# Where Silu's activation table is loaded in a fused HGRN2 attention and SwiGLU kernel

## The chip, the core and the metric

The kernel runs on one core of a Trainium2 chip. The metric is the device time of one execution in microseconds, smaller being better, given as the median over runs. Names of engines: PE is the matmul engine (TensorE), PEld its weight load, DVE the vector engine, ACT the scalar engine with its activation tables, POOL the GpSimd engine and SP the engine whose queue issues most transfers.

## The reference

Inputs are q, k, v and f_logit of shape (4, 8, 768, 48), that is batch, heads, time and head dimension, and three weight matrices of a gated feed-forward layer. The attention is a linear recurrence with a gate per channel; its output, with heads side by side, goes through the feed-forward layer.

```python
f = 1.0 / (1.0 + np.exp(-f_logit))
for t in range(S):
    state = f[:, :, t, :, None] * state + np.einsum('bhd,bhe->bhde', k[:, :, t], v[:, :, t])
    y[:, :, t] = np.einsum('bhd,bhde->bhe', q[:, :, t], state)
x = y.transpose(0, 2, 1, 3).reshape(B * S, H * D)          # (3072, 384)
g = x @ w_gate                                             # (384, 1536)
out = (g * (1.0 / (1.0 + np.exp(-g))) * (x @ w_val)) @ w_out   # (1536, 384)
```

So a sigmoid is needed for the gate f, and a Silu for the feed-forward layer. On ACT these two functions use different tables.

## The kernel before

Time is cut into six chunks of 128 steps; chunk c of batch b is a unit. The four units of a chunk make the 512 tokens of one feed-forward block, so there are six blocks, 0 to 5. While PE multiplies for block c, the attention of chunk c + 1 (and the beginning of chunk c + 2) is worked in between.

Block 0 uses plain products (lines 746 to 770). The blocks 1 to 5 (`mlp_fifteen`, lines 908 to 1028) compute gate and value with 15 products per group of columns where the plain way has 18, at the price of sums before and after. There are four such groups, called triples; each runs its products 0 to 14 in the order of the list PRODUCTS (lines 897 to 901). A product accumulates into a bank named A, B, o or c, with gate and value side by side, 512 columns. Because product 3, 6, 9, 12 and 14 all add to the same bank A, ACT first has to copy the running sum out ("aside" or "c11", "c12" and so on, line 959); DVE adds or subtracts the copies (lines 855 and 858). When one of six results is complete, `finish` (line 965) puts it on a list; later products take it off, apply Silu to the gate half on ACT (line 970) and let DVE multiply by the value half (line 906). The first two results, c12 and c22, get their Silu right after the matmuls of products 9 and 10, ahead of the copies of these products.

Then the block goes its way down (`down_seven`, lines 1030 to 1122): 14 half steps of matmuls with w_out, in which ACT only copies two results (lines 1072 and 1079) and issues two output transfers (line 1062). At its end `token_sums` (line 916) prepares on DVE the sums of tokens that the next block's products take.

The attention of a unit (`attention`, lines 528 to 704) is a generator, and each `yield` ends a step. Its first step is the sigmoid of its f logits, for chunks from 2 on in place in a room called fsquares (line 555). The next steps are transposes on DVE (561, 568, 599), scans of the gates (572, 596), the scores on PE (615), their mask on DVE (628), y on PE (649 and 653, or 674), the copy of y towards xT (657 and transfers 664, or 689), and the update of the state. There is one room each for f, k and q: the next unit's transfers are issued by `load_after` once the q transpose of the unit before is written down (line 600).

The order is written out by hand. A clock called now advances by 0.86 for each product and by 1.95 for each half step of the way down, which makes 78.9 for a block ("whole"). `times(c)` (line 835) gives for each unit of chunk c at what value of this clock each step is due, counted from the start of block c - 1, and the main loop (lines 1271 to 1280) lets the steps that are due come in ahead of the next product or half step. From a mark on (line 1248), each engine executes its instructions in that written order. What was written before the mark, the end of block 0 included, is placed by the framework's scheduler.

The first entry of each unit's due times is its sigmoid: for chunk 2 at 0, and then at the due times of the scores of the unit before; for chunk 3 at -14 for b = 0 (that is 64.9 in the block before) and 0.80 for b = 1; for the chunks 4 and 5 at -21.51 for b = 0 and -7.86 for b = 1. An activation whose function is not in the table at hand gets a table load put ahead of it, which shows in the profile as ACT_TABLE_LOAD under the line of that activation.

Of the kernel before, what the change touches and what calls it, by code (L numbers as in the profile page):

```python
# [9 lines left out]
FP32 = mybir.dt.float32  # L10
I32 = mybir.dt.int32
U32 = mybir.dt.uint32
AF = mybir.ActivationFunctionType
# [276 lines left out]
def short_path(ctx, tc, ident, least, judge, q, k, v, f_logit, moe_w_gate, moe_w_val, moe_w_out, out):  # L290
# [9 lines left out]
    nc = tc.nc  # L300
# [14 lines left out]
    SQUARES = 2  # L315
    assert TB <= 512 and DM % 128 == 0 and D <= W

    const = ctx.enter_context(tc.tile_pool(name="const", bufs=1))
# [44 lines left out]
    def pairs(t, off=0):  # L363
        return t[:, off:off + HP * N1].rearrange("p (a t) -> p a t", t=N1)
# [4 lines left out]
        nc.vector.memset(t, 1.0)  # L369
    nc.vector.memset(least, 1.0)  # L370

    states = [const.tile([128, HP, D], FP32, tag=f"state{b}", name=f"state{b}") for b in range(B)]


# [32 lines left out]
    def squares(nm):  # L407
        return rooms[nm][:, Q:Q + HP * RUN].rearrange("t (a i e) -> t a i e", a=HP, i=NI)[:, :, :, 0:Q]
# [119 lines left out]
    def attention(u):  # L528
        b, c = units[u]
# [17 lines left out]
        def transposed(name, src):  # L547
            p = bank(name)
            for a in range(HP):
                nc.tensor.transpose(p[:, a * C:(a + 1) * C],  # L550
                                    src[:, 2 * a:2 * a + 2, :].rearrange("t r d -> t (r d)"), ident)
            return p.rearrange("p (a t) -> p a t", t=C)

        if c >= SQUARES:
            nc.scalar.activation(squares("f"), squares("f"), AF.Sigmoid)
        else:
            p = transposed("fTp", fr)
            nc.scalar.activation(pairs(gate)[:, :, 1:N1], p, AF.Copy if u in ahead else AF.Sigmoid)
# [15 lines left out]
        whole = pairs(tail)[:, :, 1:2]  # L574
# [92 lines left out]
        else:  # L667
# [15 lines left out]
            for par in range(2):  # L683
                for n in range(DM // Q):
                    h = n // per * 2 + par
                    at = n * Q - h * D
# [25 lines left out]
    def attention_steps(c):  # L712

        runs = [attention(c * B + b) for b in range(B)]
        parts = [3, 6, 3, 3]
        order = sorted((2 * b + s, b, n) for b in range(B) for s, n in enumerate(parts))
        return [lambda b=b, n=n: [next(runs[b]) for _ in range(n)] for _, b, n in order]
# [101 lines left out]
    def chain(k, q, qmul, turn=None, head=None):  # L819
        return (*[k + t for t in STEPS], turn or k + 3.5, head or k + 3.5, q, qmul)  # L820

    whole = NJ * TRIPLE + 7 * DOWN
    between = [n * TRIPLE - 0.05 for n in range(NJ)]
    down = [NJ * TRIPLE + n * DOWN / 2 - 0.05 for n in range(14)]
    SCORES = {c: scores for c, scores in zip(range(2, NCH), (
        ((12, "b"), (between[2], "o"), (down[2], "A"), (down[6], "A")),
        ((PRODUCT - 0.05, "b"), (between[1], "o"), (between[3], "o"), (down[3], "A")),
        *[((down[10] - whole, "A"), (between[1], "o"), (between[3], "o"), (down[3], "A"))] * (NCH - 4)))}
# [6 lines left out]
    def times(c):  # L835
        at = [t for t, _ in SCORES[c]]
        outputs = [*at[1:], down[10] if c + 1 in SCORES and SCORES[c + 1][0][0] < -1 else LAST]
        sigmoid = [-14 if c == 3 else SCORES[c - 1][-1][0] - whole - 0.01 if c > 3 else 0, *[t - 0.01 for t in at]]
        masks = {"b": 2, "o": 0.9, "A": 1.5}
        return [[f, *steps, s + 0.02, s + masks[kind], s + 2.2, o, o + 0.01, o + 2.1]  # L840
                for f, steps, (s, kind), o in zip(sigmoid, CHAINS[c], SCORES[c], outputs)]
# [321 lines left out]
    mark = traced[-1]  # L1163
    keep_warm(5)
    first = [attention(b) for b in range(B)]
    done = [0] * B

# [82 lines left out]
    for c in range(2, NCH):  # L1250
        for b in range(B):
            run = attention(c * B + b)
            waiting += [((c - 2) * whole + t, lambda run=run: next(run)) for t in times(c)[b]]
# [33 lines left out]
def kernel(  # L1287
# [22 lines left out]
    def judge(bank):  # L1310
# [12 lines left out]
        yield  # L1323

    short_path(tc, ident, least, judge, *args)
    with tc.If(redo[0] > 0):
        general_path(tc, *args)
# [32 lines left out]
```

## Time and profile before

| | |
|---|---|
| time, median of 8 runs | 615.09 us (614.3 to 615.52) |
| the profiled execution | 615.41 us, span 613.6 us |
| PE busy | 597.0 us (97%) |
| DVE busy | 499.1 us (81%) |
| ACT busy | 285.4 us (47%), 526 instructions |
| table loads on ACT | 30, each 1283 ns: line 970 12, line 555 11, line 558 4, line 762 3 |
| starts of the blocks 1 to 4 (first product) | 147.99, 247.25, 343.26, 437.12 us |

Times within the profile are microseconds from the start of the span. A row of the timeline has the start, the duration, the engine, the line, the operation with its output and inputs, and how often it ran; in brackets stands how long the engine was idle before it and what ended this ("<-issue" where nothing in the profile did). A row of the waits names who waited for whom, the sum in us, how many times, and the longest. A row of the groups has, after the bar, busy time and the mean of one in ns, then idle time before them. The chain of waits is followed back from the last instruction to what released each one. ACTq, SPq and POOLq are the queues of those engines.

### The profile page before, as it was taken

How to read it: one execution, taken by the hardware profiler on the slowest of the kernel's cores; microseconds unless marked ns; L12 is line 12 of the kernel's file. 1: busy time of each engine (PE TensorE's matmuls, PEld its weight loads, DVE VectorE, ACT ScalarE, POOL GpSimd, SP SyncE). 2: the span in 40 equal slices, each digit the busy share in tenths (PEclk: the TensorE clock that was granted, in tenths of full speed). 3: DMA queues.
4: the chain of work that ended last, by engine and by line, in shares of the span. 5: the costliest groups of instructions: out<-in, count | busy, mean ns of one | idle time of the engine just before them, and what ended most of it. 6: DMA issues, size and time to landing. Idle time of an engine off the chain costs nothing.

```text
span 613.6 us, 10812 instructions
## 1 busy us (share of the span) xinstructions
PE 597.0 (97%) x4036; PEld 489.1 (80%) x4036; DVE 499.1 (81%) x882; ACT 285.4 (47%) x526; POOL 7.6 (1%) x51
## 2 busy tenths in 40 slices
PE   7799999999999999999999999999999999999996
PEld 5644545666888799888899988899988899988895
DVE  7799989878999996989996889996879991566731
ACT  2375646312776520576731376641276730366600
POOL 1000000000000000000000000000000000000000
PEclk9899999999999999999999999999999999999999
DMA  9999582005322144424235344145313100100001
GB/s 150 248 209 284 174 249 79 1 14 154 88 52 68 27 98 109 119 53 96 52 94 125 100 112 110 32 113 117 109 44 91 27 5 10 52 2 2 1 0 58
DMA packets 109142, 54.10 MB, mean 88 GB/s; under 512 B 68760, under 2 KB 102168, under 8 KB 109080
## 3 DMA queue, kind: packets, MB, share of 16 engines
q1 hardware_dynamic: 107064, 50.56, 34.7%
q10 hardware_dynamic: 2016, 2.75, 1.2%
q8 instruction: 34, 0.56, 0.4%
q14 instruction: 28, 0.23, 0.1%
HBM read 44.04 MB, written 6.29 MB: 82 GB/s over the span
## 4 chain that ended last, share of the span: by engine, by line
PE 83%; DVE 7%; DMA 3%; ACT 2%; SPq 2%; issue 2%; POOL 0%; DVEq 0%; ACTq 0%; POOLq 0%
PE o L1053 17%; PE A L954 14%; PE B L954 11%; PE gate L752 5%; PE o L775 5%; PE val L752 5%; PE o L954 5%; PE c L954 4%; PE sc L615 4%; PE o L1116 3%; PE y L653 2%; PE y L674 2%; PE dS L694 1%; SPq L664 1%; PE y L649 1%
## 5 line engine op out<-in xcount | busy, mean ns | idle before, releaser
L954 PE MATMUL A<-xs,w_both 128*128 128x256 f32 x240 | 62.5, 383 | 1.2 <-ACT aside L959 1.2
L1053 PE MATMUL o<-w_out,h 128*128 128x192 f32 x360 | 62.0, 327 | 0.5 <-DVE h L906 0.5
L1053 PEld LDWEIGHTS o<-w_out,h 128*128 128x128 f32 x360 | 58.7, 190 | 1.7 <-DVE h L906 0.8
L959 ACT COPY c<-A 128x512 f32<-128x512 f32 x40 | 23.4, 584 | 66.2 <-PE A L954 59.2
L954 PEld LDWEIGHTS A<-xs,w_both 128*128 128x128 f32 x240 | 44.5, 190 | 9.1 <-ACT aside L959 2.8
L855 DVE TENSOR_TENSOR c<-c,aside 128x512 f32<-128x512 f32 x60 | 41.3, 688 | 9.9 <-ACT aside L959 8.5
L959 ACT COPY aside<-A 128x512 f32<-128x512 f32 x60 | 35.0, 584 | 28.9 <-PE A L954 28.9
L906 DVE TENSOR_TENSOR h<-h,c 128x256 f32<-128x256 f32 x100 | 40.8, 417 | 7.9 <-ACT h L970 7.7
L970 ACT ACTIVATE h<-c 128x256 f32<-128x256 f32 x100 | 39.2, 416 | 9.0 <-DVE c L855 5.8
L858 DVE TENSOR_TENSOR c<-c,aside 128x512 f32<-128x512 f32 x60 | 41.1, 685 | 2.0 <-ACT aside L959 1.8
L954 PE MATMUL B<-xs,w_both 128*128 128x256 f32 x160 | 41.2, 380 | 0.7 <-ACT aside L959 0.7
L1053 PE MATMUL o<-ws,h 128*128 128x192 f32 x240 | 41.5, 328 | 0.2 <-DVE A L628 0.2
L954 PE MATMUL c<-xT,w_both 128*128 128x256 f32 x160 | 41.2, 380 | 0.5 <-DVE c L858 0.5
L954 PE MATMUL A<-xs,extra 128*128 128x256 f32 x160 | 41.2, 380 | 0.0
L954 PE MATMUL B<-xT,extra 128*128 128x256 f32 x160 | 41.1, 379 | 0.0
L959 ACT COPY aside<-B 128x512 f32<-128x512 f32 x60 | 35.1, 585 | 10.5 <-PE B L954 7.0
L628 DVE TENSOR_TENSOR A<-sc,causal 128x512 f32<-128x512 f32 x48 | 30.7, 680 | 11.1 <-PE sc L615 11.1
L1053 PEld LDWEIGHTS o<-ws,h 128*128 128x128 f32 x240 | 39.1, 190 | 0.8 <-DVE A L628 0.4
L858 DVE TENSOR_TENSOR c<-o,c 128x512 f32<-128x512 f32 x40 | 27.6, 691 | 10.2 <-ACT h L970 5.8
L954 PEld LDWEIGHTS B<-xs,w_both 128*128 128x128 f32 x160 | 30.2, 190 | 5.2 <-ACT aside L959 1.1
L954 PEld LDWEIGHTS c<-xT,w_both 128*128 128x128 f32 x160 | 30.2, 190 | 5.1 <-DVE c L858 0.9
L954 PEld LDWEIGHTS A<-xs,extra 128*128 128x128 f32 x160 | 30.3, 190 | 4.4 <-ACT c L959 0.3
(137 smaller groups left out, 1139.6 us busy)
## 6 DMA issues: line engine op xcount, KB each, us to landing
fsquares<-in_f_logit_dram SPq DMA_DIRECT2D x64, 96.0 KB, 2.7
ksquares<-in_k_dram SPq DMA_DIRECT2D x64, 96.0 KB, 2.4
qsquares<-in_q_dram SPq DMA_DIRECT2D x64, 96.0 KB, 2.4
v<-in_v_dram SPq DMA_DIRECT2D x24, 192.0 KB, 3.3
w<-in_moe_w_gate_dram SPq DMA_DIRECT2D x6, 768.0 KB, 6.1
w<-in_moe_w_val_dram SPq DMA_DIRECT2D x6, 768.0 KB, 5.7
w<-in_moe_w_out_dram SPq DMA_DIRECT2D x6, 768.0 KB, 5.7
out_dram<-ob ACTq DMA_DIRECT2D x14, 192.0 KB, 2.5
```

What stands on the lines that cost most here:

```text
L615: nc.tensor.matmul(sc[par][:, a * C:(a + 1) * C], lhsT=kT[r, a, :], rhs=qT[r, a, :], start=True, stop=True)
L628: nc.vector.tensor_tensor(A[:, par], sc[par].rearrange("p (a t) -> p a t", t=C), causal.unsqueeze(1).broadcast_to((128, HP, C)), ALU.mult)
L752: nc.tensor.matmul(p, lhsT=w[:, j, i, :], rhs=xT[c][:, i, :], start=(i == 0), stop=(i == KT - 1))
L775: nc.tensor.matmul(p, lhsT=hidden_tile(h, n // 2)[:, n % 2 * 2 + b // 2, b % 2 * C:(b % 2 + 1) * C], rhs=w_out[:, j, :], start=(n == 0), s ...
L855: nc.vector.tensor_tensor(dst, a, b, ALU.add)
L858: nc.vector.tensor_tensor(dst, a, b, ALU.subtract)
L906: lagging.append(lambda: f(*args))
L954: nc.tensor.matmul(p[name][:, n, :], lhsT=weights_of[a][:, n, j, :], rhs=tokens[b], start=fresh and n == 0, stop=True, skip_group_check=True)
L959: nc.scalar.copy(t, p[name])
L970: nc.scalar.activation(dst, src[:, 0, :], AF.Silu)
L1053: nc.tensor.matmul(p[:, n, :], lhsT=lhsTs[j][:, n * C:(n + 1) * C], rhs=rhs[:, j, :], start=first and j == order[0] and n == 0, stop=j == ...
L1116: nc.tensor.matmul(p, lhsT=hidden_tile(h, j)[:, 2, n * C:(n + 1) * C], rhs=b22[:, j, :], start=j == order[0], stop=j == order[-1])
```

## The change

A tile of one column, "spare", is allocated and zeroed on POOL. After the sigmoid of unit b = 0 of chunk 2, and of unit b = 1 of the chunks 3, 4 and 5, ACT applies Silu to this column in place; nothing reads it. The sigmoid of unit b = 1 of chunk 3 becomes due at -4 where it was due at 0.80: in the way down of block 1, no more in the first triple of block 2. For the chunks 4 and 5 the due times stay.

```diff
@@ short_path
     nc.vector.memset(least, 1.0)

+    spare = const.tile([128, 1], FP32, tag="spare", name="spare")
+    nc.gpsimd.memset(spare, 0.0)
     states = [const.tile([128, HP, D], FP32, tag=f"state{b}", name=f"state{b}") for b in range(B)]
@@ attention
         if c >= SQUARES:
             nc.scalar.activation(squares("f"), squares("f"), AF.Sigmoid)
+            if b == (c > SQUARES):
+
+                nc.scalar.activation(spare, spare, AF.Silu)
         else:
@@ times
-        sigmoid = [-14 if c == 3 else SCORES[c - 1][-1][0] - whole - 0.01 if c > 3 else 0, *[t - 0.01 for t in at]]
+        sigmoid = [-14 if c == 3 else SCORES[c - 1][-1][0] - whole - 0.01 if c > 3 else 0, -4 if c == 3 else at[0] - 0.01, *[t - 0.01 for t in at[1:]]]
```

## The prediction

> **What bounds the kernel now.** I began with the page. The profiled execution took 615.41 us; its span is 613.6, so 1.81 lie around it, and it stands 0.32 above the median of 615.09.
>
> ```profile
> ## 1 busy us (share of the span) xinstructions
> PE 597.0 (97%) x4036; PEld 489.1 (80%) x4036; DVE 499.1 (81%) x882; ACT 285.4 (47%) x526; POOL 7.6 (1%) x51
> ```
>
> TensorE is busy for 97%, ACT for less than half. A change on ACT pays only where TensorE stands still for ACT. So next the waits of TensorE, and the groups of ACT:
>
> ```profile
> PE A L954 <- ACT aside L959: 1.2, 4, 0.3
> L970 ACT ACT_TABLE_LOAD x12 | 15.4, 1283 | 0.2
> L555 ACT ACT_TABLE_LOAD x11 | 14.1, 1283 | 0.2
> ```
>
> Four times a matmul into bank A waits for the copy "aside" on ACT, for 0.3 us each time. Tables are swapped 12 times ahead of a Silu of line 970 and 11 times ahead of a sigmoid of line 555, at 1.283 us. The chain of waits, from 260 us on, is TensorE nearly throughout; it leaves it like this, and again at 445.69:
>
> ```profile
> 350.33 0.88 PE c L954 x4
> 351.84 1.14 ACT L970
> 354.07 1.13 PE A L954 x4
> ```
>
> The piece in the middle is a table load. The timeline shows how it comes between two matmuls:
>
> ```profile
> 351.23 0.59 ACT L959 COPY c<-c 128x512 f32<-128x512 f32 x1 [0.28 <-PE c L954]
> 351.55 0.67 DVE L858 TENSOR_TENSOR c<-c,aside 128x512 f32<-128x512 f32 x1
> 351.84 1.28 ACT L970 ACT_TABLE_LOAD   x1
> 352.76 1.03 PE L954 MATMUL c<-xT,w_both 128*128 128x256 f32 x4
> 353.13 0.42 ACT L970 ACTIVATE h<-c 128x256 f32<-128x256 f32 x1
> 353.46 0.57 ACT L959 COPY aside<-A 128x512 f32<-128x512 f32 x1
> 354.07 1.13 PE L954 MATMUL A<-xs,w_both 128*128 128x256 f32 x4 [0.29 <-ACT aside L959]
> 355.04 1.03 PE L954 MATMUL B<-xT,extra 128*128 128x256 f32 x4
> ```
>
> Copy of c31, load, first Silu, copy of A, all in ACT's order; product 12 adds to bank A and must let that copy read first. Starts of L954 normally lie 0.865 apart (275.82, 276.68, 277.55 for products 11 to 13 of a triple without a load). Here they are 1.31 and 0.97. The loss is 0.445 + 0.105 = 0.55 us. The same intervals (1.31 or 1.32, then 0.97) stand at 157.49, 258.43 and 446.61: four blocks' first triples, the four waits of the list.
>
> **The change, part by part.**
>
> *Load and first Silu.* The number of swaps stays; these four move from the first triple to behind the last sigmoid ahead of it. What then starts product 12? In the third block the copy of c31 ends at 351.82. The Silu needs c12 (DVE done at 350.49) and runs from 351.82 to 352.24; product 9 ends by 352.06, so the copy of A can run to about 352.8. TensorE comes to product 12 at 352.76 + 0.865 = 353.62. There are 0.8 to spare: the whole 0.55 goes. In the fourth block the rows stand alike (copy of c31 done 445.68, c12 at 443.75): 0.55. In the second, c12 comes late, from the L858 at 257.02, 0.66 long; Silu to 258.1, copy to 258.7, TensorE at 259.29. Spare is 0.6: again 0.55.
>
> What is late next there? The second Silu and the copy of B are ready before product 13. After the triple come y and scores. The second block's scores (264.74) move to 264.19, and its qT (L602, 261.80) is done by 262.48. DVE's mask at 265.93 stood idle 0.71 for those scores, more than the 0.55. In the third block DVE waits for a turn's DMA until 354.33, untouched by ACT; its qT is still done at 357.82, before scores at 358.5. Line 657's copies at 358.81 stay behind a sigmoid and do not move, but they feed DMAs, not the next product. So 3 x 0.55 = 1.65.
>
> *The first block* has a chain of its own, on DVE:
>
> ```profile
> 159.57 0.67 DVE L602 TENSOR_TENSOR qT<-qT,gates 128x512 f32<-128x512 f32 x1
> 160.72 1.16 PE L615 MATMUL sc<-qT,kT 48*128 48x128 f32 x16
> 163.45 1.12 DVE L561 STREAM_TRANSPOSE gates<-fsquares 128x512 f32<-128x512 f32 x1 [0.47 <-issue]
> ```
>
> DVE works without a gap from 155.98 to 162.98. The scores need that qT (160.24) and start at 160.36 at best, where TensorE alone could be 0.55 earlier: 0.36 stay. DVE's gap of 0.47 waits for the sigmoid of 162.73, which moves up with the copy of product 13; that can close. Between 0.36 and 0.47 I take 0.40, since both engines alternate as the bound up to 211 us. Its bounds are 0 (DVE would hold it all) and 0.55.
>
> *Four one-column Silus and the places of the loads.* The trace has no one-column activation. Copies of 256 and 512 columns take 368 and 584 ns, 0.84 per column, which leaves 0.15 us for one column; the 192-column copy's 0.35 is the upper bound. I take 0.16, since the line through two copies extrapolates by little. With the load, 1.45 us. What covers them:
>
> ```profile
> 146.26 0.48 ACT L796 COPY ob<-o 128x384 f32<-128x384 f32 x1 [3.62 <-PE o L775]
> 248.31 0.59 ACT L959 COPY c<-A 128x512 f32<-128x512 f32 x1 [7.00 <-DMA out_dram<-ob]
> 334.58 0.46 ACT L689 COPY xT<-y 128x384 f32<-128x384 f32 x1
> 427.66 0.48 ACT L689 COPY xT<-y 128x384 f32<-128x384 f32 x1 [1.28 <-PE y L674]
> ```
>
> At the first place ACT is free from 142.63 for 3.62: covered. At the second, from 241.32 for 7.00. At the third the sigmoid ends at 334.67 and the copy of xT behind it comes 1.45 later, at 336.1; its reader is the token sums on DVE at 341.09, so 5 us remain. At the fourth it slips by some 0.3 against a reader at 434.94. Cost 0. Without cover it would be 1.45 each: 5.8 at most. The opposite bound is 0; nothing here can gain.
>
> *The moved sigmoid (c = 3, b = 1).* The step holds one ACTIVATE and no DMA. On ACT it passes the first block's two output DMAs (245.19) and the copy of A (248.31); no SP or POOL instruction is passed. It now waits for its logits: SP issues them from 237.12 to 239.07, median landing 2.7, longest 6.8, so 241.8, at worst 245.9. With sigmoid, load and column (0.63 + 1.45) ACT is free at 243.9, at worst 248.0, before the 248.31 copy. The output DMAs queued behind it could slip by 2.8, and no later product reads them. Its old place was between copies with 1.30 of idle behind it: gain 0. DVE's transpose stays where its order puts it (249.64).
>
> *The memset* is one more on POOL at the start: neighbours take 0.10, and the first product does not wait for POOL, which is idle from 3.3 to 10.3. Cost 0, at most 0.1.
>
> *A rule against.* The trace has 30 loads, each 1283 ns, and the next activation starts 10 ns behind one. The Trainium skill ("ScalarE: Activation LUTs", What ACT_TABLE_LOAD costs and Rules for kernel authors) counts about 2.66 us, a drain included, for every switch, and says to group by set. As the switches stay 30, that rule alone saves nothing and adds four activations, so 615.1; with its price a load that was uncovered would cost 1.38 more than the row. No such drain is to be seen here, and the rule does not say where a switch stands.
>
> **Sum.** 1.65 + 0.40 - 0 = 2.05 us. Span 611.55, profiled execution 613.36, median 613.04.
>
> **Rivals.**
> 1. *DVE takes over the wait* (20%). In the first block its chain is in fact the bound, and in the second the Silu waits for c12 with 0.6 spare. If the first gives 0 and the second half, the gain is 0.27 + 1.1 = 1.4; if nothing holds in either, 1.1, that is 613.7 to 614.0. For it: DVE's unbroken run there. Against: its 0.47 of idle, and the 0.71 in the second block.
> 2. *The load does not land where it should* (8%). Order across the end of the plain block is not written out; the first column could come behind both output copies. Then load and column end at about 149.8, the copies of A and B slip from 149.24 and 149.92 by 0.5, and with them the DVE chain that begins at 150.84: gain 1.65 - 0.5 = 1.15, 613.9. If no load moves at all, 615.1 remains. For: the sigmoid did run ahead of earlier-written copies, so the order is chosen. Against: ACT had nothing else ready for 3.62.
> 3. *Slower: addresses* (8%). The new tile stands ahead of states, v, all weights and the sums, which may shift by a few bytes. If shifted operands cost TensorE, 2.05 / 597 = 0.34% already eats the gain; at 1% the result is 615.09 - 2.05 + 5.97 = 619.0. For: no row shows such a shift. Against: L954 takes 383, 380, 380 and 379 ns with operands in four pairs of places.
>
> **How the numbers follow.** My case, all four blocks, gets 64% and 1.65 to 2.2 us. This kernel's measurement can tell about 0.2%, 1.23 us. Faster by more: 64 plus the larger half of rival 1 (8) is 72%. Within: the rest of rival 1 (12) and rival 2 (8), 20%. Slower: 8%. The low end is 615.09 - 2.2 with the runs' spread of about 0.5 below: 612.3. The high end takes in most of rivals 1 and 2, a gain of 0.5: 614.6. Outside are rival 3, an unmoved load and the tails.
>
> **What would show it.** Right: 12 loads at L970 become 8, four stand at the new line in ACT's idle time, "PE A <- ACT aside" disappears from the waits, products 11 to 13 are 0.865 apart, and the chain has no ACT L970 piece. The step on the first block is wrong if TensorE still reaches 211 us at the same time. The cover is wrong if the copy of xT is followed by an idle DVE ahead of the token sums. All of it is wrong if product 12 still starts 1.3 behind product 11, or if rows of unchanged shapes grow longer.

## The result

The changed kernel takes 613.47 us (median of 11 runs, 612.27 to 614.47) against 615.1 for the kernel before (32 runs); the ratio is 0.997, with a 95% interval of 0.9961 to 0.9979, that is 1.3 to 2.4 us less. Twice more on other occasions the ratio was 0.9971 and 0.9977. The forecast was 613.0, in a range of 612.3 to 614.6. The profiled execution took 613.21 us, its span is 611.5.

First the engines on the page, then the groups of table loads on ACT. Five lines are added to the file, so 954 is now 959, 970 is 975, 555 is 557; 560 is the new one-column Silu.

```profile
PE 594.8 (97%) x4036; PEld 488.5 (80%) x4036; DVE 499.1 (82%) x882; ACT 286.2 (47%) x530; POOL 7.6 (1%) x52
```

```profile
L557 ACT ACT_TABLE_LOAD x11 | 14.1, 1283 | 0.2
L975 ACT ACT_TABLE_LOAD x8 | 10.3, 1283 | 0.1
L560 ACT ACT_TABLE_LOAD x4 | 5.1, 1283 | 0.1
```

ACT has four instructions and 0.8 us more. Four of the twelve loads at the Silu of `finish` went over to the new line; the sum of loads stayed 30. The row "PE A <- ACT aside" is no longer in the waits. In the timeline the place in the third block that the prediction showed now reads:

```profile
349.53 0.58 ACT L964 COPY c<-c 128x512 f32<-128x512 f32 x1 [0.27 <-PE c L959]
350.01 0.42 ACT L975 ACTIVATE h<-c 128x256 f32<-128x256 f32 x1
350.40 0.58 ACT L964 COPY aside<-A 128x512 f32<-128x512 f32 x1
351.06 1.03 PE L959 MATMUL c<-xT,w_both 128*128 128x256 f32 x4
351.92 1.03 PE L959 MATMUL A<-xs,w_both 128*128 128x256 f32 x4
352.79 1.03 PE L959 MATMUL B<-xT,extra 128*128 128x256 f32 x4
```

The Silu follows the copy of c31 at once, the copy of A ends 0.94 before product 12, and the products 11 to 13 lie 0.86 and 0.87 apart. The load has gone here (also the timeline, in the way down before it):

```profile
331.82 0.63 ACT L557 ACTIVATE fsquares<-fsquares 128x512 f32<-128x512 f32 x1 [6.93 <-DMA fsquares<-in_f_logit_dram]
332.46 1.28 ACT L560 ACT_TABLE_LOAD   x1
333.76 0.20 ACT L560 ACTIVATE spare<-spare 128x1 f32<-128x1 f32 x1
333.87 0.46 ACT L694 COPY xT<-y 128x384 f32<-128x384 f32 x1
```

The copy of xT comes 1.4 us after the sigmoid's end, and its reader, the token sums on DVE, starts at 339.39, 5 us after the end of that copy.

**Where the time came from.** To see it, I took the starts of the groups sc (scores), y and dS (update of the state) on PE in each profile and subtracted them from those of before: the lead. It grows or shrinks only where something differs. "Block 1" is from dS at 136.97 to dS at 178.12 in the times of before, "way down" from there to the scores at 248.21, "block 2" from there to y at 292.58, "block 3" from the scores at 334.27 to those at 359.07 and then to y at 386.53, "block 4" from the scores at 428.12 to y at 479.93. All are us gained on the profile of before.

| kernel (labels explained below) | up to block 1 | block 1 | way down | block 2 | block 3 | ... after | block 4 |
|---|---|---|---|---|---|---|---|
| change | 0.67 | 0.38 | 0.02 | 0.54 | 0.47 | -0.50 | 0.56 |
| change, e0 | -0.66 | 0.37 | 0.55 | 0.54 | 0.55 | -0.40 | 0.55 |
| change, e10 | 0.66 | 0.38 | 0.21 | 0.54 | 0.55 | -0.27 | 0.56 |
| e1, all but the Silus | 0.44 | 0.01 | 0.02 | -0.01 | -0.01 | 0.01 | 0.00 |
| e2, first block only | 0.43 | 0.38 | 0.15 | -0.01 | 0.00 | 0.00 | 0.00 |
| e4, own staging | -0.82 | 0.41 | 0.36 | 0.54 | 0.55 | 0.00 | 0.55 |
| e9, own staging | -0.53 | 0.39 | 0.54 | 0.54 | 0.55 | 0.00 | 0.56 |
| e5, before with own staging | 0.27 | 0.00 | 0.23 | -0.01 | 0.00 | 0.00 | 0.00 |
| e3, two loads in the triple | -0.34 | -1.52 | 0.14 | -1.53 | -1.51 | 0.00 | -1.51 |
| e6, one more pair | 0.71 | -1.15 | 0.17 | 0.54 | 0.55 | 0.00 | 0.55 |
| e8, pair at three places | -0.26 | 0.38 | -0.25 | 0.54 | 0.49 | -0.50 | 0.55 |
| e7, three more pairs | 0.52 | -8.73 | -0.45 | -1.60 | -2.97 | 0.00 | -1.62 |

In the profile of the change the lead reaches 2.23. But 0.67 of it stood before block 1, where only the memset of the new tile differs. In the windows from 20 to 26 us the two executions differ in something else; the columns after the stretch and its length are PE, PEld, DVE, ACT and POOL busy (with counts), granted clock, DMA share and GB/s. First before, then the change:

```profile
20.00:26.00 6.00, 5.58 (x75) 4.68 (x76) 3.10 (x8) 1.43 (x4) 0.11 (x1) 0.72 1.02 256
```

```profile
20.00:26.00 6.00, 5.38 (x104) 4.70 (x108) 4.41 (x10) 2.74 (x6) 0.10 (x1) 1.00 1.01 226
```

TensorE was granted 0.72 of its clock there in the one and 1.00 in the other. This belongs to the execution and not to the kernel: the changed kernel had 0.66 from 21 to 26 us in e0, and 1.00 in e10. So I count for the change only the rest: 0.38 + 0.54 + 0.47 - 0.50 + 0.56 = 1.45 in this profile, 1.6 in e0 and 1.8 in e10 (the way down, which also varies between kernels without the change, left out). That agrees with the 1.3 to 2.4 of the timed runs.

### The profile page after: what moved, and what is told of

It is laid out like the page before. It is cut to its first block, busy times and chain, and to the rows that moved or that the text cites. A ratio compares the mean times of both kernels' runs of the same rounds, so it can differ in the third digit from the quotient of the medians.

```text
span 611.5 us, 10816 instructions
## 1 busy us (share of the span) xinstructions
PE 594.8 (97%) x4036; PEld 488.5 (80%) x4036; DVE 499.1 (82%) x882; ACT 286.2 (47%) x530; POOL 7.6 (1%) x52
## 4 chain that ended last, share of the span: by engine, by line
PE 68%; DVE 9%; ACT 3%; issue 3%; SPq 2%; DMA 2%; POOL 0%; DVEq 0%; ACTq 0%; POOLq 0%
PE o L1058 17%; PE A L959 14%; PE B L959 11%; PE o L780 5%; PE o L959 5%; PE c L959 5%; PE sc L620 3%; PE o L1121 3%; PE y L658 2%; PE y L679 1%; DVE c L863 1%; SPq L669 1%; PE y L654 1%; DVE c L860 1%; PE dS L699 1%
```

## The experiments

**Theory:** TensorE stood still in four first triples because a load came between two copies; 0.55 us come back where TensorE is the bound, and less where DVE is. **Rivals:** it is the new tile or the moved sigmoid; DVE takes the wait over; a load costs its time wherever it stands.

**e1, all but the Silus.**

```diff
-            if b == (c > SQUARES):
-
-                nc.scalar.activation(spare, spare, AF.Silu)
```

> The change without the one-column Silus: the tile, its memset and the moved sigmoid stay, so the loads stand where they stood. Theory: no gain, ratio 0.999 to 1.001; the four intervals of 1.31 us ahead of product 12 are back. Rival addresses or moved sigmoid: a difference of more than 1 us to the kernel before, with shapes on TensorE that take longer or shorter than before.

Measured: 614.52, ratio 1.0006 (0.9995 to 1.0018). The waits show the old row:

```profile
PE A L956 <- ACT aside L961: 1.2, 4, 0.3
```

The table has nothing above 0.01 in any block. Tile, memset and moved sigmoid are worth nothing by themselves; the gain needs the Silus.

**e2, the first block alone.**

```diff
-            if b == (c > SQUARES):
+            if b == 0 and c == SQUARES:
...
-        sigmoid = [..., -4 if c == 3 else at[0] - 0.01, *[t - 0.01 for t in at[1:]]]
+        sigmoid = [..., *[t - 0.01 for t in at]]
```

> Only the first of the four Silus is kept (chunk 2), the sigmoid of chunk 3 stays at its old place. Theory: TensorE gains 0.36 to 0.40 between product 11 and the end of the triples of block 1, no more, since the scores then wait for DVE's qT; the blocks 2 to 4 show 1.31 again; time 614.7, ratio 0.9990 to 0.9998. Rival (DVE holds all of block 1): lead 0 at the end of block 1's triples. Rival (TensorE keeps the whole 0.55): lead 0.55 there.

Measured: 614.94, ratio 1.0002 (0.9986 to 1.0017), which is too coarse for 0.4 us. The profile is not: the lead grows by 0.38 in block 1 and by nothing in the other three. What limits it stands in the same profile:

```profile
157.93 1.03 PE L959 MATMUL A<-xs,w_both 128*128 128x256 f32 x4
158.79 1.03 PE L959 MATMUL B<-xT,extra 128*128 128x256 f32 x4
159.98 1.16 PE L620 MATMUL sc<-qT,kT 48*128 48x128 f32 x16 [0.17 <-DVE qT L607]
```

Products 12 and 13 keep their pace, and then the scores wait for DVE's qT, a wait that was not there before.

**e0 and e10, the change again,** beside the others.

> The changed kernel once more, as the partner of the others on this chip. Theory (four loads taken out of TensorE's wait): the first product-12 interval of each of the blocks 1 to 4 is 0.865 us, and the time is 1.3 to 2.2 us below the kernel before (ratio 0.9965 to 0.998). Rival (the lead of 0.67 us that the profile showed already at the start of block 1 belongs to the change): block 1 starts at about 147.3 again in every execution of the change, and at 148.0 in every execution of the old order.

> The change again as the partner of both. Theory: block 3 gains 0.55 and gives back 0.4 to 0.6 at the scores of its second unit, as in both profiles so far; time 1.3 to 2.2 us below the kernel before.

Measured: 613.22 (ratio 0.9971, 0.9961 to 0.9982) and 613.04 (0.9977, 0.9967 to 0.9988). Against the rival named for e0, block 1 started 0.66 later than in the kernel before, not earlier. Block 3 gave back 0.40 and 0.27; the lower end that I expected was 0.4.

**e4 and e9, the change with a staging room of its own.** In block 3 the scores of the second unit of chunk 4 are late. In the profile of the change:

```profile
353.23 1.14 DVE L604 STREAM_TRANSPOSE qT<-qsquares 128x512 f32<-128x512 f32 x1 [2.71 <-DMA turn<-qT]
356.02 0.73 DVE L607 TENSOR_TENSOR qT<-qT,gates 128x512 f32<-128x512 f32 x1
356.62 0.73 DVE L863 TENSOR_TENSOR c<-c,c 128x512 f32<-128x512 f32 x1
356.90 1.66 PE L620 MATMUL sc<-qT,kT 48*128 48x128 f32 x16
358.49 1.13 PE L959 MATMUL A<-xs,w_both 128*128 128x256 f32 x4
```

The 16 score matmuls take 1.66 where they took 1.16. In the profile before, the same place reads:

```profile
357.74 0.68 DVE L858 TENSOR_TENSOR c<-c,c 128x512 f32<-128x512 f32 x1
359.07 1.16 PE L615 MATMUL sc<-qT,kT 48*128 48x128 f32 x16
```

These scores go into two banks of the pool that the products o and c use, and the second is free only when DVE's subtraction c<-c,c has read bank c. In the change the trace has the third of the 16 matmuls at 357.41, 0.06 after the end of that subtraction, which it waited for. So the scores started 0.08 later than the lead of y would have had them, right behind qT (done at 356.75), and lost 0.50 between their first and third matmul, because of the subtraction. In e0, e10 and e8 the third matmul likewise starts 0.05 to 0.06 after it. The subtraction follows qT on DVE, and both follow the q transpose.

The q transpose has to wait, because the room that it writes, qT, still feeds a transfer: the decayed keys are staged in it on their way to DRAM and back ("turn"). The edit stages them elsewhere, for this one unit:

```diff
-            beside = qT.rearrange("p a t -> p (a t)").rearrange("p (i m) -> p i m", i=NI)
+            staged = qT if u != 4 * B + 1 else att.tile([128, HP, C], FP32, tag="x", name="own")
+            beside = staged.rearrange("p a t -> p (a t)").rearrange("p (i m) -> p i m", i=NI)
```

> The change, and unit b = 1 of chunk 4 stages its turn in the room named x in place of its own qT, so that the q transpose on DVE in block 3 has no turn transfer to wait for. Theory (block 3 gives its 0.55 back because DVE waits for the turn and so hands qT and the o bank to the scores late): DVE's 2.7 us of idle ahead of that transpose is gone, the product after the scores follows them by 1.09 and not 1.59, and the time is 0.5 below the change. Rival (the scores wait for something else, such as the mask or the bank alone): the gap of 1.59 stays, and the time is that of the change.

> The change with the own staging room for unit b = 1 of chunk 4, again, beside the change itself. Theory: 0.4 to 0.6 us below the change; TensorE keeps its 0.55 through block 3.

Measured: 612.54 (ratio 0.9963, 0.995 to 0.9977) and 612.81 (0.9968, 0.9956 to 0.998). In the profile of e4:

```profile
351.54 1.20 DVE L605 STREAM_TRANSPOSE qT<-qsquares 128x512 f32<-128x512 f32 x1
354.36 0.74 DVE L608 TENSOR_TENSOR qT<-qT,gates 128x512 f32<-128x512 f32 x1
357.93 1.16 PE L621 MATMUL sc<-qT,kT 48*128 48x128 f32 x16
359.02 1.13 PE L960 MATMUL A<-xs,w_both 128*128 128x256 f32 x4
```

DVE no longer idles ahead of the transpose, the scores take 1.16 again, and the product after them follows by 1.09. The lead of block 3 stays in both profiles. With 15 runs the median is 612.72, with the 22 of e0 and e10 613.22; the 0.5 is the size that was expected, but the intervals overlap, so that the times alone do not prove it. It is the fastest version tried.

**e5, the same staging in the kernel before.** Same edit.

> The kernel before with only the own staging room for unit b = 1 of chunk 4. Theory: DVE's wait for the turn was not what set the end while the table load stood in block 3, so no gain: ratio 0.999 to 1.001. Rival (the staging is worth something by itself): 0.5 us or more below the kernel before.

Measured: 615.3, ratio 1.0001 (0.9992 to 1.0009), and 0.00 in block 3. DVE's wait for the turn cost nothing as long as the load stood in the triple; it came to bear with the load gone.

**e3, two loads where one was.**

```diff
                 product(r)
+                if r == 9 and j == 0 and c < NCH - 1:
+                    nc.scalar.activation(spare, spare, AF.Sigmoid)
                 if r in FINISH and late:
```

> The change, and in the first triple of the blocks 1 to 4 a one-column sigmoid ahead of the Silu of product 9, so that two loads (sigmoid's and Silu's again) stand where one stood before. Theory (a load there costs TensorE what it exceeds the slack by): copy of A ends 1.28 + 0.2 us later than in the kernel before, so each block loses 0.55 + 1.5 = 2.0 us against the change; four blocks 8, so about 621.5 (620 to 622.5). Rival (loads are mostly taken up by other waits): less than 3 us above the change.

Measured: 621.23, ratio 1.01 (1.0083 to 1.0118). The third block in its timeline:

```profile
355.00 1.28 ACT L982 ACT_TABLE_LOAD   x1
355.92 1.03 PE L959 MATMUL c<-xT,w_both 128*128 128x256 f32 x4
356.29 0.20 ACT L982 ACTIVATE spare<-spare 128x1 f32<-128x1 f32 x1
356.51 1.28 ACT L975 ACT_TABLE_LOAD   x1
357.81 0.42 ACT L975 ACTIVATE h<-c 128x256 f32<-128x256 f32 x1
358.13 0.57 ACT L964 COPY aside<-A 128x512 f32<-128x512 f32 x1
358.75 1.13 PE L959 MATMUL A<-xs,w_both 128*128 128x256 f32 x4 [1.80 <-ACT aside L964]
```

One load costs TensorE 0.55, two and a column 0.55 + 1.52, in each of the four blocks. Of the first load's 1.28 some 0.7 are hidden; of the second nothing is. From one activation past a load to the next is 1.52 us (356.29 to 357.81), so no drain beyond the 1.283 shows. The Trainium skill ("ScalarE: Activation LUTs", What ACT_TABLE_LOAD costs) counts 2.66 per switch, a drain included; by an estimate from that page each switch would have cost 1.4 more here.

**e6, e8 and e7, more loads at the covered places.**

```diff
-                nc.scalar.activation(spare, spare, AF.Silu)
+                for f in (AF.Silu, AF.Sigmoid) * 1 + (AF.Silu,):      # e6; e7: * 3
+                    nc.scalar.activation(spare, spare, f)
```

e8 is e6 with the pair only where c > SQUARES.

> The change with one more pair behind each of the four one-column Silus: a one-column sigmoid and Silu again, so two more loads and columns, 2.97 us more on ACT at each place, 8 loads more in all. Theory (the places are covered): no cost, time that of the change, 613.0 to 613.8, though ACT is busy for 11.9 us more. Rival (a switch costs wherever it stands): up to 11.9 us more, 625.

Measured: 615.15, ratio 0.9999 (0.9991 to 1.0008). Not covered, then: 1.7 above the first measurement of the change, though on another occasion. The table says where: the blocks 2 to 4 have their full 0.54 and 0.55, but block 1 lost 1.15 where the change gains 0.38. Its first place, in the timeline of e6:

```profile
141.49 1.28 ACT L561 ACT_TABLE_LOAD   x1
142.78 0.20 ACT L561 ACTIVATE spare<-spare 128x1 f32<-128x1 f32 x1
145.55 0.48 ACT L802 COPY ob<-o 128x384 f32<-128x384 f32 x1 [2.56 <-PE o L781]
146.05 1.28 ACT L561 ACT_TABLE_LOAD   x1
147.45 0.46 ACT L802 COPY ob<-o 128x384 f32<-128x384 f32 x1
148.93 1.28 ACT L561 ACT_TABLE_LOAD   x1 [1.01 <-DVE ob L802]
150.33 0.57 ACT L965 COPY c<-A 128x512 f32<-128x512 f32 x1
```

Only the first column stands behind the sigmoid. The framework put the second between the two output copies of block 0 and the third behind them, although ACT idled for 2.56 us in between. So the third load runs into block 1's first copy. The change's own load is safe there by the framework's choice of place, not by the order that the code writes down.

> One more pair (sigmoid and Silu on the column, two loads more) at the second, third and fourth place only, none at the first, where the earlier kernel with a pair everywhere lost 1.5 us because the framework had put the pair behind the copies of block 0's outputs. Theory (order written out and idle time there): six loads more cost nothing, the time is that of the change. Rival (each switch costs somewhere): up to 6 x 1.48 = 8.9 us more.

Measured: 613.74, ratio 0.9983 (0.9968 to 0.9997). Six loads and columns, 9 us more of ACT, and the blocks show what the change shows. The median is 0.7 above that of e10 beside it, but the intervals of the two ratios overlap. At the three places whose order is written out, one more pair of loads is free.

> The change with three more pairs at each place, 8.9 us more on ACT each. Theory: now the cover is used up at all four. Counted from the profile of the change: block 1's first copies slip to about 153.5, 4.3 late for product 3; block 2's to 252.7, 2.9 late; in block 3 the copy of xT ends at 343.3, 4.0 late for the token sums; in block 4 at 435.8, 2.6 late. Sum 13.7: about 627 (624 to 629). Rival (the copy of xT has no reader in a hurry): blocks 3 and 4 give nothing, 620 to 621.

Measured: 630.3, ratio 1.0244 (1.0229 to 1.0259), 3 us more than expected. Against the change the blocks 2 to 4 lost 2.1, 3.5 and 2.2, where 2.9, 4.0 and 2.6 were expected; the copies of xT have readers after all once the slack is used. Block 1 lost 9.1 where 4.3 were expected, and that has two parts in the profile of e7. Six of the seven loads stand behind block 0's first output copy, five of them behind both, so that PE waits 6.97 for the copy of A (from 150.2 to 157.20): the reason seen in e6. And the clock granted to TensorE falls to a mean of 0.66 from 156 to 164 us; the starts of the products 3 to 6 lie 1.87, 1.71 and 1.16 apart in place of 0.865, another 2.15. So about two of the three us that the forecast missed come from the clock. The dip began during that idle time of PE (0.82 from 152 to 156); that the idle time caused it is not shown.

## Why the prediction was right, point by point

- *The 0.55 of the blocks 2 to 4.* Measured 0.54 to 0.56 at each place, in every profile with the load moved and covered; the 0.47 of the change and the 0.49 of e8 in block 3 already hold a part of what was given back. That it was read from the intervals of TensorE (1.31 and 0.97 against 0.865), and not from the 1.283 of a load, made it exact.
- *The first block.* 0.40 forecast between bounds of 0 and 0.55, measured 0.37 to 0.41: 0.31 to 0.35 at the scores, limited by their wait for qT as said, and some 0.06 behind them. So here rival 1 was weighed correctly inside the sum.
- *The cover.* The column took 0.20, forecast 0.16 between 0.15 and 0.35. The moved sigmoid started at 240.90 (241.8 forecast, in the times of before, which this profile leads by 1.07 there), and ACT was free again at 243.04, ahead of the output transfers at 244.12. At the first place the cover held in the change, but rival 2 was nearer than its 8% suggested: e6 shows the framework placing the added loads behind the output copies, though not the first one.
- *The step that failed* is the sentence on the third block: "DVE waits for a turn's DMA until 354.33, untouched by ACT; its qT is still done at 357.82, before scores at 358.5". Two things in it failed. First, it counted the slack to qT alone, 0.7. The scores also waited for the subtraction c<-c,c, which ended at 358.42 in the profile before: with the scores 0.55 earlier, at 358.52, the slack was 0.1. Second, it took the landing of the turn from one profile. From the first issue of that turn to the q transpose it was 5.18 in the profile before, 5.78, 5.54, 5.43 and 5.75 in the change, e0, e10 and e8, but 4.81 and 4.65 in e6 and e7, which stage in qT as well and gave nothing back. Where a load still stands in block 3's triple (before, e1, e2, e3) it ranges as widely, from 4.64 to 5.86, so nothing here ties it to the change. Counted from the start of block 3's lead, the subtraction ended 0.63, 0.45, 0.32 and 0.61 later in the change, e0, e10 and e8 than before, and these gave back 0.58, 0.40, 0.27 and 0.56 from the peak of the lead: the lateness less some 0.05 of slack. That term was missing from the sum. It is rival 1's mechanism, but in the block in which I had called it safe. The sum with it is 0.38 + 3 x 0.55 less about 0.4, or 1.6; e4 and e9, without the give-back, come to 2.05, the number forecast. As the give-back runs from nothing to 0.58 by the execution, it is partly luck that the measured median lies only 0.4 above the forecast.
- *The rival of addresses* fell with e1. *The rule that counts switches* gave no gain; the switches did stay 30 and the time fell, since their places decide.

Left open: why the turn lands early in some executions and late in others. DVE's operations of 512 columns there took 0.73 to 0.79 in the change and 0.73 to 0.75 in e4, against 0.68 before, for a reason that is open too; it cost little, since qT and the subtraction behind it start 0.60 apart in all of them.

## What to carry to other kernels

A table load costs what it delays, not what it takes: find the loads that a full engine waits behind, read the loss from that engine's own intervals, and let an activation of one column draw the load into idle time. Then follow every engine that now has less slack for one block further, its DMAs included, and take a transfer's landing as a range and not as the one duration of one profile. Where the order across a border is left to a scheduler, the cover belongs to that schedule.

## What was not expected of the hardware

In some executions the clock granted to TensorE, taken as the mean from 21 to 26 us, is only 0.59 to 0.71, in others 1.00, with the same kernel (the change: 0.66 in e0, 1.00 in e10). The six profiles with this dip (before, e0, e3, e4, e8, e9) come to block 1 with a lead of -0.82 to 0. In e5 the dip comes later (0.57 from 30 to 34 us), and its lead there is 0.27. The six without a dip ahead of block 1 (the change, e1, e2, e6, e7, e10) have 0.43 to 0.71. So up to 1.5 us between two single profiles have nothing to do with the edit; they can be compared by stages, but not by their spans. What sets the dip off is not known from these runs.
